# The two halves of every moving row of two MLPs are set 8 columns out of a 64-column step

## The chip, the core and the metric

The kernel runs on one core of one Trainium2 chip. Its engines are TensorE (PE for the matrix products, PEld for loading the stationary operand), VectorE (DVE), ScalarE (ACT), GpSimd (POOL) and SyncE (SP, which issues the DMAs). They work on SBUF, a memory of 128 partitions; PSUM holds the results of the matrix products. A column is here four bytes of a partition. The metric is the time of one execution on the chip in microseconds, the median over runs: 617.85 us before the change, from three runs of 614.94, 617.85 and 618.59 us.

## What is computed

Attention over a sliding window with a few sinks, and behind it two MLPs on the 1536 tokens:

```python
a = softmax(where(is_sink | in_window, q @ k.T / sqrt(64), -1e9))   # 2 batches, 8 heads, 768 tokens
x = (a @ v) as 1536 x 512
h = x @ w_in;  g = h * clip(h + 3, 0, 6) / 6;       x = g @ w_out    # first MLP, 512 -> 2048 -> 512
h = x @ w_in2; g = h / (1 + exp(-1.702 * h));       return g @ w_out2
```

All of it is in float32.

## The kernel before

**Exact products from three.** PE takes operands of the type F32R. Each float32 operand of the MLPs is split into a high part (a cast to F32R, by `copy`, lines 428 to 432) and a low part (the float32 value less the high one, a subtraction on VectorE), and each product is three matmuls: high by high, high by low, low by high. So x stands in `xyh` and `xyl` (lines 141 and 142, three blocks of 512 tokens each, four chunks of 128 features by 512 columns), a tile of W_in in `w0h` and `w0l`, a tile of W_out in `w1h` and `w1l`, and g in `gh` and `gl` (512 columns each).

**The stages.** The work is a list of 96 items: an item is one of 16 tiles of 128 inner features, for one block of 512 tokens, in one of the two MLPs. `up` (line 529) splits W_in's tile and makes 12 matmuls of 512 columns (four chunks by three products, line 541) into a bank of PSUM, forms u = h times its gate from it, and splits u into `gh` and `gl` (lines 578 to 587). `down` (line 592) makes 12 more (line 609) with W_out's parts. In the first MLP `gh` and `gl` are moving and W_out stationary there; in the second it is the other way round. `result` (line 625) writes x for the second MLP back into `xyh` and `xyl`.

**Moving rows.** A moving row of 512 columns is not read from left to right: `woven` (line 434) reads it as column 0, column 256, column 1, column 257 and so on, the two halves in turn. The results come out in that order, and W_out of the second MLP and the output's rows are laid out accordingly.

```python
    def woven(x):
        return x.rearrange("p (a n) -> p n a", a=2)
```

Every such row starts at a multiple of 64 columns in SBUF: two unused tiles, `gap_x` of 40 columns ahead of `xyh` and `gap_w` of 72 ahead of the MLP's tiles, see to that.

**Unpacking the weights.** A tile of weights comes by DMA as 2048 columns of 32-bit words into one of two `stage` tiles; a low and a top word of each weight stand side by side. `plan_convert` (line 445) makes 1024 float32 weights of it in `wf`, in five operations: the absolute value of the top words on ScalarE (L452), a clamp and a shift with a mask on `wf` (L457, L465), and two operations that take the top and then the low words in (L473, L480), these four on VectorE. L452, L473 and L480 read `stage` with a step of two columns:

```python
        wd = st.tile.rearrange("p (n t) -> p n t", t=2)
        low, top = wd[:, :, 0], wd[:, :, 1]
```

The 16 tiles of the first MLP are unpacked while the attention still runs, those of the second during the last items of the first MLP. From `wf` each item splits what it needs anew.

**What sets the order.** `Plan` collects operations with their reads, writes, the engines that may take them and an estimated cost, and `issue` (line 354) puts them out engine by engine in an order that follows from these costs and due times. Each engine works through its own list in that order. Tiles used in turn are rings of buffers (`mlp_rings`, line 679).

## Time and profile before

| | us |
|---|---|
| median of 3 runs (lowest, highest) | 617.85 (614.94, 618.59) |
| profiled execution | 615.07 |
| its span, first to last instruction | 613.3 |
| PE busy with matmuls | 586.0 |
| VectorE busy | 451.3 |
| ScalarE busy | 360.8 |
| mean share of PE's clock granted | 0.992 |

The span is the part of the execution from the first to the last instruction of the trace. Busy time is the time in which at least one instruction of the engine was under way. Consecutive matmuls overlap, and the mean time of one is longer than its distance from the next; the distance is read by counting matmuls in a stretch without gaps. A count with x in front belongs to the group or stretch; in a stretch it includes instructions that its ends cut. The sign <- behind an idle time names what ended it.

### The profile page before, as it was taken

To read this page: it belongs to the slowest core of one execution; us is meant where nothing else is said; L and a number is where in the kernel's file an instruction comes from. 1 tells how busy PE (TensorE), PEld (TensorE's weight loads), DVE (VectorE), ACT (ScalarE), POOL (GpSimd) and SP (SyncE) were. 2 spreads that over 40 slices of the span, in tenths; PEclk is the share of its full clock that TensorE was granted. 3 is DMA by queue.
4 is the path that set the end of the run, shared out by engine and by line. 5 is a ranking of instruction groups with operands and counts; after the bars stand their busy time and mean duration, and the time that the engine had idled before them with its cause. 6 is when DMAs were issued, how large, how long until landed. Compare 5 with 4: busy or idle time off the path is not lost.

```text
span 613.3 us, 10624 instructions
## 1 busy us (share of the span) xinstructions
PE 586.0 (96%) x4242; PEld 500.3 (82%) x4242; DVE 451.3 (74%) x896; ACT 360.8 (59%) x718; POOL 1.4 (0%) x10
## 2 busy tenths in 40 slices
PE   6889999999999999999999999999999999999995
PEld 6778777787878888888878877888888888888884
DVE  7799999999995665499999999945455455455541
ACT  5897776865765764475666575544644444544442
POOL 0000000000000000000000000000000000000000
PEclk9899999999999999999999999999999999999998
DMA  8974344244430000003444334000100000200002
GB/s 265 373 231 150 131 137 155 97 160 166 131 134 1 1 2 2 0 1 137 138 137 138 137 113 161 3 0 1 51 18 0 2 1 1 69 0 1 0 1 73
DMA packets 11175, 50.91 MB, mean 83 GB/s; under 512 B 1456, under 2 KB 1456, under 8 KB 7024
## 3 DMA queue, kind: packets, MB, share of 16 engines
q1 hardware_dynamic: 11120, 50.18, 24.6%
q8 instruction: 35, 0.57, 0.4%
q14 instruction: 20, 0.16, 0.1%
HBM read 47.02 MB, written 3.15 MB: 82 GB/s over the span
## 4 chain that ended last, share of the span: by engine, by line
PE 53%; DVE 30%; ACT 6%; DMA 6%; issue 5%; POOL 0%; SPq 0%; DVEq 0%; ACTq 0%; POOLq 0%
PE bank L609 24%; PE bank L541 24%; DMA stage<-in_w_dram 5%; DVE wf L480 5%; DVE wf L473 4%; DVE w1l L522 3%; DVE w0l L522 3%; DVE gl L584 3%; DVE u L558 3%; DVE wf L457 2%; ACT pexp L779 2%; ACT wf L452 2%; DVE wf L465 2%; DVE pexp L771 2%; PE bank L756 1%
## 5 line engine op out<-in xcount | busy, mean ns | idle before, releaser
L541 PE MATMUL bank<-xyh,w0h 128*128 128x512 f32 x384 | 147.1, 383 | 0.5 <-ACT xyh L430 0.5
L541 PE MATMUL bank<-xyl,w0h 128*128 128x512 f32 x384 | 145.7, 379 | 1.0 <-DVE xyl L857 1.0
L541 PE MATMUL bank<-xyh,w0l 128*128 128x512 f32 x384 | 145.7, 379 | 0.2 <-DVE w0l L522 0.2
L522 DVE TENSOR_TENSOR w1l<-wf,w1h 128x512 fp32r<-128x512 f32 x96 | 66.0, 687 | 56.9 <-ACT w1h L430 56.9
L430 ACT CAST w1h<-wf 128x512 fp32r<-128x512 f32 x90 | 55.6, 618 | 58.5 <-PE bank L609 57.7
L430 ACT CAST gh<-u 128x512 fp32r<-128x512 f32 x91 | 56.3, 619 | 44.4 <-DVE u L558 24.8
L541 PEld LDWEIGHTS bank<-xyl,w0h 128*128 128x128 f32 x384 | 72.6, 189 | 11.1 <-DVE xyl L857 1.3
L541 PEld LDWEIGHTS bank<-xyh,w0h 128*128 128x128 f32 x384 | 72.6, 189 | 10.9 <-issue 0.6
L541 PEld LDWEIGHTS bank<-xyh,w0l 128*128 128x128 f32 x384 | 72.6, 189 | 10.8 <-DVE w0l L522 0.6
L609 PE MATMUL bank<-gl,w1h 128*128 128x512 f32 x192 | 74.4, 388 | 4.0 <-DVE gl L584 3.7
L609 PE MATMUL bank<-w1h,gl 128*128 128x512 f32 x192 | 73.4, 382 | 2.0 <-DVE gl L584 1.9
L609 PE MATMUL bank<-gh,w1h 128*128 128x512 f32 x192 | 75.0, 391 | 0.2
L609 PE MATMUL bank<-w1h,gh 128*128 128x512 f32 x192 | 72.9, 380 | 0.0
L609 PE MATMUL bank<-w1l,gh 128*128 128x512 f32 x192 | 72.8, 379 | 0.0
L609 PE MATMUL bank<-gh,w1l 128*128 128x512 f32 x192 | 72.8, 379 | 0.0
L584 DVE TENSOR_TENSOR gl<-u,gh 128x512 fp32r<-128x512 f32 x96 | 66.2, 689 | 7.0 <-ACT gh L430 2.7
L572 DVE TENSOR_TENSOR u<-bank,u 128x512 f32<-128x512 f32 x48 | 32.9, 685 | 47.5 <-ACT u L567 47.5
L522 DVE TENSOR_TENSOR w0l<-wf,w0h 128x512 fp32r<-128x512 f32 x96 | 65.5, 682 | 1.7 <-ACT w0h L430 1.5
L567 ACT ACTIVATE u<-bank 128x512 f32<-128x512 f32 x48 | 28.7, 598 | 57.1 <-PE bank L541 57.1
L452 ACT ACTIVATE wf<-stage 128x1024 f32<-128x1024 f32 x32 | 47.1, 1472 | 20.2 <-DMA stage<-in_w_dram 19.2
L430 ACT CAST w0h<-wf 128x512 fp32r<-128x512 f32 x84 | 51.4, 612 | 0.7 <-DVE wf L480 0.4
L553 ACT ACTIVATE u<-bank,three 128x512 f32<-128x512 f32 x48 | 32.8, 684 | 31.7 <-PE bank L541 31.6
(93 smaller groups left out, 817.4 us busy)
## 6 DMA issues: line engine op xcount, KB each, us to landing
stage<-in_w_dram SPq DMA_DIRECT2D x32, 1024.0 KB, 5.0
wf<-in_kq_dram SPq DMA_DIRECT2D x8, 520.0 KB, 11.1
vc<-in_vc_dram SPq DMA_DIRECT2D x12, 320.0 KB, 6.6
out_dram<-u SPq DMA_DIRECT2D x12, 256.0 KB, 2.9
vb<-in_v_dram SPq DMA_DIRECT2D x10, 256.0 KB, 6.6
kq<-in_kq_dram SPq DMA_DIRECT2D x4, 520.0 KB, 10.8
vb<-in_v_dram SPq DMA_DIRECT2D x4, 128.0 KB, 6.4
par_i<-in_params_dram SPq DMA_DIRECT2D x1, 2.0 KB, 3.0
```

Source lines behind the costliest of these rows:

```text
L430: eng.copy(out, in_)
L452: lambda e: e.activation(w.tile.bitcast(F32), top.bitcast(F32), AF.Abs),
L473: lambda e: e.scalar_tensor_tensor(out=w.tile, in0=top, scalar=-0x40000000, in1=w.tile, op0=ALU.bitwise_and, op1=ALU.bitwise_or),
L480: lambda e: e.scalar_tensor_tensor(out=w.tile, in0=low, scalar=29, in1=w.tile, op0=ALU.logical_shift_right, op1=ALU.bitwise_or),
L522: lambda e: e.tensor_tensor(out=lo.tile, in0=src.tile.bitcast(F32)[:, cols], in1=hi.tile.bitcast(F32), op=ALU.subtract),
L541: e.matmul(h.tile[:, :n], w, woven(x), start=(c == 0 and k == 0), stop=(c == NC - 1 and k == 2))
L553: lambda e: e.activation(u.tile[:, :n], h.tile[:, :n], AF.Relu, bias=three, scale=1.0),
L558: lambda e: e.scalar_tensor_tensor(out=u.tile[:, :n], in0=u.tile[:, :n], scalar=6.0, in1=h.tile[:, :n], op0=ALU.min, op1=ALU.mult,),
L567: lambda e: e.activation(u.tile[:, :n], h.tile[:, :n], AF.Sigmoid, scale=1.702),
L572: lambda e: e.tensor_tensor(out=u.tile[:, :n], in0=h.tile[:, :n], in1=u.tile[:, :n], op=ALU.mult),
L584: lambda e: e.tensor_tensor(out=gl.tile[:, :n], in0=u.tile[:, :n], in1=gh.tile[:, :n].bitcast(F32), op=ALU.subtract),
L609: e.matmul(yb.tile, l, woven(r), start=(begin and k == 0), stop=(end is not None and k == 2))
```

## The change

x moves into one tile, `xy`, and W_out's parts and g's parts into one tile, `wg`. Each has two planes, one for the first halves of all rows and one for the second halves. The planes lie a multiple of 64 columns and 8 more apart: 6144 + 8 = 6152 columns in `xy` (six high and low blocks by four chunks by 256), 2048 + 8 = 2056 in `wg` (eight buffers of 256). Before, the two halves of a row lay 256 columns apart. `xy` begins at a multiple of 64 columns like `xyh` before it, `wg` at 16 columns more, and the other tiles behind `xy` move by 16 or 32 columns.

What writes these tiles now writes two pieces of 256 columns instead of one of 512 (four pieces of 128 from the attention, as before). A stationary operand of 128 columns out of them lies within one plane (`quarter`). Numbers, engines, estimated costs and the order of the instructions are as before on all five engines. W_in's parts `w0h` and `w0l`, which are stationary only, keep their form.

```diff
+APART = 8
...
     const.tile([P, 40], F32, name="gap_x")
-    xyh = [const.tile([P, NC, 512], F32R, name=f"xyh{s}") for s in range(NBLK)]
-    xyl = [const.tile([P, NC, 512], F32R, name=f"xyl{s}") for s in range(NBLK)]
+    xy = const.tile([P, 2, 2 * NBLK * NC * 256 + APART], F32R, name="xy")
+    xyh, xyl = (
+        [
+            xy[:, :, (2 * s + k) * NC * 256 : (2 * s + k + 1) * NC * 256].rearrange("p a (c n) -> p a c n", c=NC)
+            for s in range(NBLK)
+        ]
+        for k in range(2)
+    )
     landed = {}
...
     def woven(x):
-        return x.rearrange("p (a n) -> p n a", a=2)
+        return x.rearrange("p a n -> p n a")
+
+    def parted(x):
+
+        return x.rearrange("p (a n) -> p a n", a=2)
+
+    def quarter(x, e4):
+
+        return x[:, e4 // 2, e4 % 2 * P : (e4 % 2 + 1) * P]
     def halves(t0, n):
         return range(t0 // 256, (t0 + n) // 256)
...
             hi, lo = Buf(cls=f"w{part}h"), Buf(cls=f"w{part}l")
             cols = slice(512 * part, 512 * (part + 1))
             src = plan.wf[f]
+            of = lambda: parted(src.tile.bitcast(F32)[:, cols]) if part else src.tile.bitcast(F32)[:, cols]
             when = None
             plan.op(
                 to_act,
-                lambda e: copy(e, hi.tile, src.tile.bitcast(F32)[:, cols]),
+                lambda e: copy(e, hi.tile, of()),
                 when, reads=[src], writes=[hi], chain=f"split{part}",
             )
             plan.op(
                 [("DVE", 602)],
                 lambda e: e.tensor_tensor(
-                    out=lo.tile, in0=src.tile.bitcast(F32)[:, cols], in1=hi.tile.bitcast(F32), op=ALU.subtract
+                    out=lo.tile, in0=of(), in1=hi.tile.bitcast(F32), op=ALU.subtract
                 ),
                 when, reads=[src, hi], writes=[lo],
             )
...
             which, t0, n, f = items[i][:4]
             wh, wl = split(i, 0)
             h = Buf(cls="bank", kind="h")
-            s, o = divmod(t0, 512)
+            s = t0 // 512
+            assert n == 512 and t0 % 512 == 0
             for c in range(NC):
                 def mm(e, c=c):
-                    xh, xl = xyh[s][:, c, o : o + n], xyl[s][:, c, o : o + n]
+                    xh, xl = xyh[s][:, :, c, :], xyl[s][:, :, c, :]
                     cols = slice(c * P, (c + 1) * P)
                     prods = ((wh.tile[:, cols], xh), (wh.tile[:, cols], xl), (wl.tile[:, cols], xh))
                     for k, (w, x) in enumerate(prods):
...
                 )
             plan.op(
                 [("ACT", 520)] if i >= second - NF + 4 else [("ACT", 520), ("DVE", 335)],
-                lambda e: copy(e, gh.tile[:, :n], u.tile[:, :n]),
+                lambda e: copy(e, gh.tile, parted(u.tile)),
                 after, reads=[u], writes=[gh],
             )
             plan.op(
                 [("DVE", 602 if big else 335)],
                 lambda e: e.tensor_tensor(
-                    out=gl.tile[:, :n], in0=u.tile[:, :n], in1=gh.tile[:, :n].bitcast(F32), op=ALU.subtract
+                    out=gl.tile, in0=parted(u.tile), in1=gh.tile.bitcast(F32), op=ALU.subtract
                 ),
                 after, reads=[u, gh], writes=[gl],
             )
...
                 yb = ys["b"][e4]
                 def mm(e, e4=e4, yb=yb):
-                    col = slice(e4 * P, (e4 + 1) * P)
                     if which == 1:
-                        a, b = wh.tile[:, col], wl.tile[:, col]
+                        a, b = quarter(wh.tile, e4), quarter(wl.tile, e4)
                         prods = ((a, gh.tile), (b, gh.tile), (a, gl.tile))
                     else:
-                        prods = ((gh.tile[:, col], wh.tile), (gh.tile[:, col], wl.tile), (gl.tile[:, col], wh.tile))
+                        a, b = quarter(gh.tile, e4), quarter(gl.tile, e4)
+                        prods = ((a, wh.tile), (a, wl.tile), (b, wh.tile))
                     for k, (l, r) in enumerate(prods):
                         e.matmul(yb.tile, l, woven(r), start=(begin and k == 0), stop=(end is not None and k == 2))
...
         def result(which, t0, e4, yb, when):
             if which == 1:
                 s = t0 // 512
-                hi, lo = xyh[s][:, e4, :], xyl[s][:, e4, :]
+                hi, lo = xyh[s][:, :, e4, :], xyl[s][:, :, e4, :]
                 his = [plan.x[half][e4][0] for half in halves(t0, 512)]
                 los = [plan.x[half][e4][1] for half in halves(t0, 512)]
                 if (t0, e4) in kept_y:
...
                         when, reads=[psum], writes=[part],
                     )
                     yb = part
-                plan.op([("ACT", 478)], lambda e: e.mul(hi, yb.tile, 1.0 / 6.0), when, reads=[yb], writes=his)
+                plan.op([("ACT", 478)], lambda e: e.mul(hi, parted(yb.tile), 1.0 / 6.0), when, reads=[yb], writes=his)
                 plan.op(
                     [("DVE", 602)],
                     lambda e: e.scalar_tensor_tensor(
-                        out=lo, in0=yb.tile, scalar=1.0 / 6.0, in1=hi.bitcast(F32), op0=ALU.mult, op1=ALU.subtract,
+                        out=lo, in0=parted(yb.tile), scalar=1.0 / 6.0, in1=hi.bitcast(F32), op0=ALU.mult, op1=ALU.subtract,
                     ),
                     when, reads=[yb] + his, writes=los,
                 )
...
         down(len(items) - 1)
     def mlp_rings(plan, pool, psum):
+        parts = (("w1h", 2), ("w1l", 2), ("gh", NG), ("gl", NG))
+        n = sum(n for _, n in parts)
+        wg = pool.tile([P, 2, n * 256 + APART], F32R, name="wg")
+        k0 = 0
+        for cls, n in parts:
+            plan.ring(cls, n, lambda k, k0=k0: wg[:, :, (k0 + k) * 256 : (k0 + k + 1) * 256])
+            k0 += n
         for cls, n, cols, dt in (
-            ("w0h", 2, 512, F32R), ("w0l", 2, 512, F32R), ("w1h", 2, 512, F32R),
-            ("w1l", 2, 512, F32R), ("u", NU, 512, F32), ("gh", NG, 512, F32R), ("gl", NG, 512, F32R), ("aside", 4, 512, F32),
+            ("w0h", 2, 512, F32R), ("w0l", 2, 512, F32R), ("u", NU, 512, F32), ("aside", 4, 512, F32),
         ):
             plan.ring(cls, n, lambda k, cls=cls, cols=cols, dt=dt: pool.tile([P, cols], dt, name=cls, tag=f"{cls}{k}"))
         plan.ring("bank", 8, lambda k: psum.tile([P, 512], F32, name="bank", tag=f"bank{k}"))
...
                 [("PE", 2000)], values, when, reads=list(dict.fromkeys([rows] + halves_of)) + pts, writes=[av],
             )
             blk, off = divmod(T, 4)
-            dst = (slice(None), slice(None), slice(off * P, (off + 1) * P))
+            dst = (slice(None), off // 2, slice(None), slice(off % 2 * P, (off % 2 + 1) * P))
             late = when + 500
             src = lambda: av.tile.rearrange("p (n t) -> p n t", n=NPAIR)
             his = [plan.x[T // 2][c][0] for c in range(NC)]
```

No instruction stands elsewhere than before; two excerpts show what is different in a row. The first is VectorE's list where a weight tile of the first MLP is unpacked, before (`gl` is the low part of g, `w1h` and `w1l` are W_out's parts; in brackets the engines waited for):

```order
L473 SCALAR_TENSOR_TENSOR wf_66<-stage_60,wf_66 128x1024 [waits DMAHW7_49]
L584 TENSOR_TENSOR gl<-u,gh 128x512 [waits Activation_49]
L480 SCALAR_TENSOR_TENSOR wf_66<-stage_60,wf_66 128x1024 [waits DVE_49]
L457 TENSOR_SCALAR wf_67<-wf_67 128x1024
L432 CAST w1h<-wf_66 128x512 [waits DVE_49,PE_49]
```

The same place after it, with the line numbers of the changed kernel:

```order
L489 SCALAR_TENSOR_TENSOR wf_66<-stage_60,wf_66 128x1024 [waits DMAHW7_49]
L602 TENSOR_TENSOR wg<-u,wg 128x2x256 [waits Activation_49]
L496 SCALAR_TENSOR_TENSOR wf_66<-stage_60,wf_66 128x1024 [waits DVE_49]
L473 TENSOR_SCALAR wf_67<-wf_67 128x1024
L440 CAST wg<-wf_66 128x2x256 [waits DVE_49,PE_49]
```

Only the tile and the shape of what is written differ. The second is PE's list after the change, in the first MLP at the start of a sum over tiles of inner features, whose four banks of PSUM are written for the first time here:

```order
L627 MATMUL bank<-wg 128x512 [waits Activation_49]
L627 MATMUL bank<-wg 128x512
L627 MATMUL bank<-wg 128x512 [waits DVE_49]
L627 MATMUL bank<-wg 128x512 [waits PE_49]
L627 MATMUL bank<-wg 128x512 x5
L627 MATMUL bank<-wg 128x512 [waits PE_49]
```

The waits of PE on its own earlier matmuls are new there; the path that runs has eight of them more than before, each on a matmul 31 to 73 matmuls back.

## Rows read from the trace of the kernel before

**Rows 1.** The page: busy time and share by engine, clock by slice.
```profile
PE 586.0 (96%) x4242; PEld 500.3 (82%) x4242; DVE 451.3 (74%) x896; ACT 360.8 (59%) x718; POOL 1.4 (0%) x10
...
PEclk9899999999999999999999999999999999999998
```
**Rows 2.** Five stretches of the span: busy us (instructions) by engine, granted clock, DMA.
```profile
core 0: us, PE busy (x) PEld busy (x) DVE busy (x) ACT busy (x) POOL busy (x), PEclk, DMA share, GB/s
0.00:41.00 41.00, 32.37 (x754) 28.74 (x754) 31.53 (x152) 31.77 (x104) 1.42 (x10) 0.92 0.91 300
41.00:180.00 139.00, 132.91 (x1389) 109.03 (x1384) 135.38 (x312) 97.48 (x223) 0.00 (x0) 1.00 0.43 142
180.00:264.00 84.00, 83.70 (x565) 72.30 (x566) 49.19 (x104) 49.31 (x103) 0.00 (x0) 1.00 0.02 9
264.00:395.00 131.00, 125.65 (x567) 105.54 (x566) 130.44 (x170) 82.69 (x120) 0.00 (x0) 1.00 0.33 113
395.00:613.30 218.30, 211.37 (x980) 184.65 (x978) 104.78 (x161) 99.50 (x171) 0.00 (x0) 0.99 0.05 15
```
**Rows 3.** Two stretches of the second MLP, same columns.
```profile
420.00:500.00 80.00, 80.00 (x373) 70.06 (x372) 41.43 (x64) 38.72 (x67) 0.00 (x0) 1.00 0.04 14
500.00:580.00 80.00, 80.00 (x372) 70.09 (x371) 39.52 (x61) 37.34 (x65) 0.00 (x0) 1.00 0.05 14
```
**Rows 4.** Groups from 264 to 395 us: busy us, mean ns, idle before, releaser.
```profile
L609 PE MATMUL bank<-gl,w1h 128*128 128x512 f32 x68 | 26.7, 392 | 3.4 <-DVE gl L584 3.4
...
L452 ACT ACTIVATE wf<-stage 128x1024 f32<-128x1024 f32 x16 | 24.5, 1532 | 9.3 <-DMA stage<-in_w_dram 8.4 <-DVE w1l L522 0.8
L480 DVE SCALAR_TENSOR_TENSOR wf<-stage,wf 128x1024 int32<-128x1024 int32 x16 | 24.5, 1528 | 0.1
L473 DVE SCALAR_TENSOR_TENSOR wf<-stage,wf 128x1024 int32<-128x1024 int32 x16 | 24.3, 1521 | 0.3
...
L430 ACT CAST gh<-u 128x512 fp32r<-128x512 f32 x23 | 14.2, 618 | 18.8 <-DVE u L558 12.4 <-DVE u L572 6.3
...
L609 PE MATMUL bank<-w1h,gl 128*128 128x512 f32 x26 | 10.4, 399 | 2.0 <-DVE gl L584 1.9
```
**Rows 5.** Operations by line, min/median/max ns: gl; w0l twice, w1l; L457 twice.
```profile
L584 DVE TENSOR_TENSOR gl<-u,gh x96: 655/691/760, 49.5 to 603.2; 128x512 fp32r<-128x512 f32 x96
...
L522 DVE TENSOR_TENSOR w0l<-wf,w0h x19: 656/681/732, 289.4 to 391.3; 128x512 fp32r<-128x512 f32 x19
...
L522 DVE TENSOR_TENSOR w1l<-wf,w1h x31: 684/692/693, 419.9 to 573.4; 128x512 fp32r<-128x512 f32 x31
...
L522 DVE TENSOR_TENSOR w0l<-wf,w0h x31: 679/681/691, 421.1 to 576.5; 128x512 fp32r<-128x512 f32 x31
...
L457 DVE TENSOR_SCALAR wf<-wf x2: 661/674/686, 23.8 to 36.3; 128x1024 f32<-128x1024 f32 x2
...
L457 DVE TENSOR_SCALAR wf<-wf x13: 668/684/733, 295.3 to 386.8; 128x1024 f32<-128x1024 f32 x13
```
**Rows 6.** The reads of stage, same columns: outside the stream, in it, whole run.
```profile
L480 DVE SCALAR_TENSOR_TENSOR wf<-stage,wf x3: 1216/1218/1222, 32.7 to 53.4; 128x1024 int32<-128x1024 int32 x3
...
L480 DVE SCALAR_TENSOR_TENSOR wf<-stage,wf x14: 1505/1523/1590, 292.7 to 391.9; 128x1024 int32<-128x1024 int32 x14
...
L473 DVE SCALAR_TENSOR_TENSOR wf<-stage,wf x14: 1498/1518/1545, 290.0 to 389.3; 128x1024 int32<-128x1024 int32 x14
...
L473 DVE SCALAR_TENSOR_TENSOR wf<-stage,wf x32: 1215/1506/1581, 26.1 to 389.3; 128x1024 int32<-128x1024 int32 x32
...
L452 ACT ACTIVATE wf<-stage x2: 1147/1163/1179, 19.7 to 28.7; 128x1024 f32<-128x1024 f32 x2
...
L452 ACT ACTIVATE wf<-stage x7: 1293/1604/1642, 305.9 to 350.3; 128x1024 f32<-128x1024 f32 x7
```
**Rows 7.** Writes in four pieces and in one; VectorE's casts. Same columns.
```profile
L857 DVE TENSOR_TENSOR xyl<-bank,xyh x12: 673/680/692, 19.4 to 216.0; 128x512 fp32r<-128x512 f32 x12
...
L642 DVE SCALAR_TENSOR_TENSOR xyl<-bank,xyh x8: 675/684/692, 223.8 to 359.5; 128x512 fp32r<-128x512 f32 x8
...
L432 DVE CAST w0h<-wf x12: 395/419/470, 34.2 to 178.3; 128x512 fp32r<-128x512 f32 x12
L432 DVE CAST w1h<-wf x6: 416/420/427, 73.2 to 188.0; 128x512 fp32r<-128x512 f32 x6
L432 DVE CAST gh<-u x5: 395/419/422, 48.9 to 180.9; 128x512 fp32r<-128x512 f32 x5
```
**Rows 8.** Groups of the whole run by line: busy us, mean ns, idle before, releaser.
```profile
L480 DVE SCALAR_TENSOR_TENSOR wf<-stage,wf 128x1024 int32<-128x1024 int32 x32 | 47.3, 1479 | 0.2
L452 ACT ACTIVATE wf<-stage 128x1024 f32<-128x1024 f32 x32 | 47.1, 1472 | 20.2 <-DMA stage<-in_w_dram 19.2 <-DVE w1l L522 0.8
L473 DVE SCALAR_TENSOR_TENSOR wf<-stage,wf 128x1024 int32<-128x1024 int32 x32 | 46.7, 1460 | 0.3
```

More of the change, by code (lines that the diff above doesn't have):

```diff
@@ L689, in put_x @@
         blk, off = divmod(T, 4)
-        dh = xyh[blk][:, :, off * P : (off + 1) * P]
+        at = (slice(None), off // 2, slice(None), slice(off % 2 * P, (off % 2 + 1) * P))
+        dh = xyh[blk][at]
         nc.scalar.copy(dh, x)
         nc.vector.tensor_tensor(
-            out=xyl[blk][:, :, off * P : (off + 1) * P], in0=x, in1=dh.bitcast(F32), op=ALU.subtract
+            out=xyl[blk][at], in0=x, in1=dh.bitcast(F32), op=ALU.subtract
         )
```

## The prediction

> **What bounds the kernel now.** [...] One busy share over stages hides who waits, so I cut the span into five stretches [rows 2]. In three of them PE sets the time: from 180 to 264 us and from 395 us to the end it is busy nearly throughout while VectorE is at about half. In the other two it is VectorE: from 41 to 180 us it is busy 135.4 of 139.0 us, from 264 to 395 us 130.4 of 131.0 us, and PE has gaps. These are the two stretches in which the 16 weight tiles of each MLP are unpacked from `stage` (L452 on ScalarE, L457 to L480 on VectorE).
>
> Next I asked what a 512-column matmul costs where nothing disturbs it [rows 3]: 745 in 160 us, 0.215 us each. [...] In the stretch from 264 to 395 us 567 matmuls begin or end, which is 121.9 us of the 131.0: PE lacks 9.1 us there, and what it waits for is `gl`, written by VectorE [rows 4].
>
> Is anything slowed by PE's reading? I compared operations inside the matmul stream with the same ones outside it. Most do not change: `w0l` takes a median of 681 ns in both MLP stretches, `gl` 655 to 760 over the whole run, the contiguous 1024-column clamp L457 674 ns without the stream and 684 with it [rows 5]. Three lines do change, and they are the ones that read `stage` with a step of two columns: L480 takes 1218 ns without the stream and 1523 with it, L473 1518 with it (its minimum, 1215, is L480's), the Abs L452 1163 without and 1604 with it [rows 6].
>
> **A reading of that stretch.** VectorE's 512-column operation takes 681 ns and its 1024-column one 1218, so 537 ns are for 512 columns and 144 are fixed. A strided read of one tile passes over 2048 columns of `stage`: without the stream in 1218 - 144 = 1074 ns, 1.91 columns per ns; in the stream in 1523 - 144 = 1379 ns, 1.49 per ns. PE passes 256 columns of each half in 215 ns, 1.19 per ns. If PE's two halves keep one place of a 64-column cycle occupied, a faster reader that catches up is held behind it, and gets past once per matmul, in the seam between two: then it gains 64 columns per matmul, (256 + 64) / 215 = 1.49 per ns. That is the row's speed. ScalarE's Abs, with the same 144 ns (no row gives its own), goes at 2.01 free and 1.40 held. Two readers of unlike speed brought to nearly the same one is what holding would look like. An operation slower than 1.19 per ns, as all 512-column ones are (512 / 537 = 0.95), never runs up from behind, and those are not stretched. L457 passes 1024 columns in about 540 ns and is not stretched either, which speaks against this reading unless it reads in two parts. [...]
>
> **The change part by part.** No instruction is added, removed or moved on any engine. Eight matmuls of the path that runs get a wait of PE on itself (the excerpt in the section on the change); each waits for a matmul 31 or more before it, 31 x 0.215 = 6.7 us earlier, so it is long met: 0. Three waits of VectorE on PE fall away, which another wait had covered: 0. `xy` and `wg` end 16 columns later each; the fixed `w0h`, `u` and mask tiles shift by 16 or 32 columns. No row shows an effect of that; 0.
>
> *Writes in two pieces.* Casts and subtractions now write 2 x 256 columns. The nearest rows are L857, which writes 4 x 128 (median 680), against L642, which writes 512 in one piece (684): no price [rows 7]. VectorE's fast cast (420 ns) has no row with pieces: 11 of its 23 casts (`w1h`, `gh`) write into `wg`. From below 0, from above the 684 ns of the slower kind, 11 x 0.264 = 2.9 us. I take 0, as pieces cost L857 nothing.
>
> *The strided reads.* This is the term that decides. Excess now: L480 47.3 us and L473 46.7 us against 32 x 1.218 = 39.0 each is 8.3 + 7.7 = 16.0 us of VectorE; L452 47.1 against 32 x 1.163 = 37.2 is 9.9 us of ScalarE [rows 8]. From 264 to 395 us it is 24.5 + 24.3 - 39.0 = 9.8 us of VectorE and 24.5 - 18.6 = 5.9 of ScalarE [rows 4], so the first unpacking holds 6.2 and 4.0. With the halves 8 columns apart in the 64-column cycle, each of two places gets half of PE's reads where one got all. No row has such halves. Bounds: the excess goes wholly (free speed), or a reader is held by both places and no longer gets past (1.19 per ns: 2048 / 1.19 + 144 = 1865 ns, +342 each). I take the first: a place that PE reads in every second column leaves the other to the reader, and the rows show no sign that PE's reading closes a place for longer than its own access, since 512-column operations, which PE overtakes, pay at most 10 ns.
>
> *What it is worth.* From 264 to 395 us VectorE would fall to 130.4 - 9.8 = 120.6 us, just below PE's 121.9; so PE becomes the bound and at most its 9.1 us come back. With two engines that close, in-order waits between them remain (ScalarE's cast of `gh` waits 18.8 us for `u` there [rows 4]); I take 7. From 41 to 180 us VectorE is busy 97%, its 6.2 us bound the gain, and part of PE's gaps there belong to the attention's short matmuls; I take 4.5. ScalarE's share lies beside VectorE's, 0. Elsewhere PE sets the time: 0. Sum 11.5 us: the profiled execution, 615.07 us with 613.3 of span, would come to 603.6. It stands 2.8 us under the median of the runs shown, 617.85, so the forecast for a median is 606.
>
> **The rivals.** *No effect.* The stretch could be a share of the memory's rate taken by PE, wherever its halves lie: both readers end near 1.4 to 1.5 columns per ns, which a fixed share would also do. For it: the figure of one lap per matmul may be chance. Against: contiguous readers pay nothing. Time 618. [...]
>
> *Half the effect.* The reader still loses a little at each of two places: half of 11.5, time 612.
>
> *Two closed places (slower).* If any read by PE closes a place, two are closed, and the seam between matmuls is too short to get past both. L473 and L480 rise by 342 ns: 32 x 0.342 = 10.9 us in the second unpacking, where VectorE is the bound; in the first, 6.2 us of excess at 305 each are 20 wholly covered reads, 7 us, of which 5 reach the end. Time 634. It decides from about 0.13 us more per read.
>
> *PE itself slows.* Every matmul row of this trace has its halves in step; out of step is not shown. 2304 matmuls give 2.3 us per ns, so 3 ns more would make it slower by over 1%. For it there is only the absence of a row; at 5 ns, time 629 if nothing else moved.
>
> **How the numbers follow.** The whole effect 0.50 (606), half 0.12 (612), none 0.18 (618), two closed places 0.13 (634), a slower PE 0.07. About 1%, 6.2 us, is what a measurement here tells from no change. Faster by over 1% is under 611.7: the first case, 0.50. Within 1%: half and none, 0.30. Slower: 0.20. The range leaves out the last two: up to 621, no effect with the casts' 2.9 us; down to 600, where all 9.1 us of the second stretch, all 6.2 of the first and some of ScalarE's 4.0 come back. The likeliest case alone runs from 600 to 610.
>
> **What would show it.** L480 and L473 near 1218 ns and L452 near 1163 from 290 to 395 us; 512-column matmuls still at 0.215 us; VectorE no longer at 99% from 264 to 395 us, PE without gaps there; casts at 420 ns. It is wrong if the three strided lines keep their 1.5 and 1.6 us, if they exceed 1.8, or if matmuls in an undisturbed stretch take longer than 0.215 us.

## The result and the profile after

The changed kernel takes 601.54 us (median of four runs, 600.42 to 602.81) where the kernel before, on the same chip, takes 617.12 (four runs): a ratio of 0.9751, 95% interval 0.9714 to 0.9788. That is faster by 15.6 us, inside the predicted range and 4.5 us below the predicted 606. The profiled execution took 602.81 us, with a span of 601.0.

The page of the changed kernel, busy time by engine and the chain that ended last:

```profile
span 601.0 us, 10621 instructions
...
PE 580.4 (97%) x4242; PEld 502.5 (84%) x4242; DVE 435.8 (73%) x896; ACT 352.4 (59%) x718; POOL 1.4 (0%) x10
...
PE 83%; DVE 8%; ACT 4%; DMA 3%; issue 1%; POOL 0%; SPq 0%; POOLq 0%; ACTq 0%
```

Against [rows 1] VectorE lost 15.5 us of work and ScalarE 8.4, with as many instructions (896 and 718). The predicted excess was 16.0 and 9.9. The lines that read `stage` (L452, L473 and L480 are now L468, L489 and L496), groups of the changed kernel's whole run, as in [rows 8]:

```profile
L489 DVE SCALAR_TENSOR_TENSOR wf<-stage,wf 128x1024 int32<-128x1024 int32 x32 | 39.1, 1222 | 0.3
L496 DVE SCALAR_TENSOR_TENSOR wf<-stage,wf 128x1024 int32<-128x1024 int32 x32 | 39.1, 1221 | 0.2
L468 ACT ACTIVATE wf<-stage 128x1024 f32<-128x1024 f32 x32 | 37.9, 1186 | 16.9 <-DMA stage<-in_w_dram 13.5 <-DMA vb<-in_v_dram 2.5 <-DVE wg L539 0.8
```

They now cost beside the matmul stream what they cost without it in [rows 6] (1218 and 1163 ns); of Abs's excess 0.02 us a tile is left. The five stretches of the changed kernel, columns as in [rows 2]:

```profile
core 0: us, PE busy (x) PEld busy (x) DVE busy (x) ACT busy (x) POOL busy (x), PEclk, DMA share, GB/s
0.00:41.00 41.00, 32.64 (x748) 29.02 (x749) 31.46 (x151) 31.84 (x104) 1.42 (x10) 0.92 0.91 300
41.00:180.00 139.00, 133.79 (x1411) 112.27 (x1408) 133.18 (x327) 98.13 (x235) 0.00 (x0) 1.00 0.45 147
180.00:264.00 84.00, 84.00 (x565) 73.06 (x564) 49.09 (x96) 48.37 (x95) 0.00 (x0) 1.00 0.00 1
264.00:395.00 131.00, 131.00 (x608) 114.36 (x607) 123.87 (x175) 80.39 (x125) 0.00 (x0) 1.00 0.32 113
395.00:601.00 206.00, 198.95 (x922) 173.74 (x920) 98.20 (x151) 93.66 (x162) 0.00 (x0) 0.99 0.06 16
```

From 264 to 395 us PE has no gap left. It runs 608 matmuls there instead of 567, 41 more at 0.215 us, which is 8.8 us. VectorE is busy for 123.87 us of the 131 although more instructions fall into the stretch: it no longer sets the time. By 264 us the changed kernel has run 748 + 1411 + 565 = 2724 matmuls, the kernel before 2708. After 395 us both are without a matmul for about the same time, 6.9 us before and 7.1 after. So of the 12.3 us between the two spans 8.8 came from the second unpacking and 3.5 from what lies before it. The matmuls themselves did not change: 372 in the 80 us from 420 to 500, as in [rows 3].

```profile
420.00:500.00 80.00, 80.00 (x372) 70.07 (x371) 39.76 (x61) 37.10 (x64) 0.00 (x0) 1.00 0.05 14
```

### The profile page after: what moved, and what is told of

Same layout as the page of the kernel before. It is cut to its first block, busy times and chain, and to the rows that moved or that the text cites. A ratio compares the mean times of both kernels' runs of the same rounds, so it can differ in the third digit from the quotient of the medians.

```text
span 601.0 us, 10621 instructions
## 1 busy us (share of the span) xinstructions
PE 580.4 (97%) x4242; PEld 502.5 (84%) x4242; DVE 435.8 (73%) x896; ACT 352.4 (59%) x718; POOL 1.4 (0%) x10
## 4 chain that ended last, share of the span: by engine, by line
PE 83%; DVE 8%; ACT 4%; DMA 3%; issue 1%; POOL 0%; SPq 0%; POOLq 0%; ACTq 0%
PE bank L627 38%; PE bank L559 38%; DMA stage<-in_w_dram 3%; PE bank L781 2%; PE bank L832 2%; ACT pexp L804 2%; PE bank L855 2%; PE bank L863 1%; DVE wf L489 1%; DVE wf L496 1%; DVE pexp L796 1%; DVE u L576 1%; PE heat L178 1%; DVE wg L602 1%; DVE wg L539 1%
## 5 line engine op out<-in xcount | busy, mean ns | idle before, releaser
L627 PE MATMUL bank<-wg 128*128 128x512 f32 x1152 | 285.4, 381 | 1.5 <-ACT wg L438 1.3
L627 PEld LDWEIGHTS bank<-wg 128*128 128x128 f32 x1152 | 215.6, 189 | 34.4 <-ACT wg L438 2.0
L559 PE MATMUL bank<-xy,w0h 128*128 128x512 f32 x768 | 230.3, 381 | 1.5 <-DVE xy L882 1.0
L559 PEld LDWEIGHTS bank<-xy,w0h 128*128 128x128 f32 x768 | 143.9, 189 | 22.2 <-DVE xy L882 1.3
L559 PE MATMUL bank<-xy,w0l 128*128 128x512 f32 x384 | 145.5, 379 | 0.0
L539 DVE TENSOR_TENSOR wg<-wf,wg 128x512 fp32r<-128x512 f32 x96 | 66.1, 689 | 57.6 <-ACT wg L438 57.6
L559 PEld LDWEIGHTS bank<-xy,w0l 128*128 128x128 f32 x384 | 72.6, 189 | 10.3
L438 ACT CAST wg<-u 128x512 fp32r<-128x512 f32 x91 | 56.3, 619 | 31.7 <-DVE u L590 17.4
L602 DVE TENSOR_TENSOR wg<-u,wg 128x512 fp32r<-128x512 f32 x96 | 66.2, 689 | 6.9 <-ACT wg L438 2.7
L468 ACT ACTIVATE wf<-stage 128x1024 f32<-128x1024 f32 x32 | 37.9, 1186 | 16.9 <-DMA stage<-in_w_dram 13.5
L489 DVE SCALAR_TENSOR_TENSOR wf<-stage,wf 128x1024 int32<-128x1024 int32 x32 | 39.1, 1222 | 0.3
L496 DVE SCALAR_TENSOR_TENSOR wf<-stage,wf 128x1024 int32<-128x1024 int32 x32 | 39.1, 1221 | 0.2
```

Of the source, the lines that this page charges most:

```text
L438: eng.copy(out, in_)
L468: lambda e: e.activation(w.tile.bitcast(F32), top.bitcast(F32), AF.Abs),
L489: lambda e: e.scalar_tensor_tensor(out=w.tile, in0=top, scalar=-0x40000000, in1=w.tile, op0=ALU.bitwise_and, op1=ALU.bitwise_or),
L496: lambda e: e.scalar_tensor_tensor(out=w.tile, in0=low, scalar=29, in1=w.tile, op0=ALU.logical_shift_right, op1=ALU.bitwise_or),
L539: lambda e: e.tensor_tensor(out=lo.tile, in0=of(), in1=hi.tile.bitcast(F32), op=ALU.subtract),
L559: e.matmul(h.tile[:, :n], w, woven(x), start=(c == 0 and k == 0), stop=(c == NC - 1 and k == 2))
```

## The experiments

Four questions were open: whether the place of the halves does it or the new tiles; whether a read is held behind TensorE's reads or only gets a smaller share of a rate; which engine's reads are worth the time; and how far apart the halves must be. Each ratio is to the kernel before as it ran on the same chip (616.59, 616.53 or 615.64 us), and the brackets give its 95% interval.

**Back in step, new tiles kept.** The distance in the 64-column cycle goes back to zero and all else of the change stays.

```diff
-APART = 8
+APART = 0
```

> The changed kernel with 0 columns instead of 8: two planes, one tile for x and one for W_out's and g's parts, all halves a multiple of 64 columns apart. HOLDING: the reads of stage are back at 1.52 us (VectorE) and 1.60 us (ScalarE), the time at 617, ratio to the kernel before 0.998 to 1.003. TILES (the gain comes from the one tile, its writes in two planes or the shifted neighbours): the reads stay at 1.22 and 1.19 us and the time at 602.

Measured: 617.13 us, ratio 1.0006, 95% interval 0.9992 to 1.0020. Time and reads are back at what they were, as the holding theory had it:

```profile
L496 DVE SCALAR_TENSOR_TENSOR wf<-stage,wf 128x1024 int32<-128x1024 int32 x32 | 47.3, 1477 | 0.2
L489 DVE SCALAR_TENSOR_TENSOR wf<-stage,wf 128x1024 int32<-128x1024 int32 x32 | 46.9, 1465 | 0.3
L468 ACT ACTIVATE wf<-stage 128x1024 f32<-128x1024 f32 x32 | 46.8, 1463 | 21.0 <-DMA stage<-in_w_dram 20.0 <-DVE wg L539 0.8
```

So the whole gain is that of the 8 columns. The writes in two pieces, the planes in one tile and the changed waits are worth nothing that ten runs can see. The reads are what comes and goes with the gain.

**The read by itself.** A probe runs a stream of woven matmuls and, beside it, three reads of `stage` for each setting (its code, shortened):

```python
for d in (0, 1, 2, 4, 6, 8, 12, 16, 32, 48, 56, 60, 64, 72, 128, 192):
    m = const.tile([P, 2, 256 + d], F32R)           # halves 256 + d columns apart
    ...                                             # 33 matmuls on m, woven
    scalar_tensor_tensor(out=o, in0=stage.rearrange("p (n t) -> p n t", t=step)[:, :, step - 1], ...)
```

> No part of the kernel: a probe that leaves attention and MLPs out. A stream of matmuls with woven rows of known distance between the halves (256 columns and 0 to 192 more), and beside it three reads of a 2048-column tile at a time, by VectorE (the operation of L473) or ScalarE (Abs). HOLDING (PE's halves keep one place of 8 columns in a 64-column cycle occupied; a faster reader is held and gets past once per matmul): VectorE's step-2 read 1.52 us at 0, 64, 128 and 192 columns apart, 1.22 at 8, 12, 16, 32, 48, 56 and 72; at 1, 2, 4, 6 and 60 in between, in proportion to the overlap (1.49, 1.45, 1.37, 1.30, 1.37). In step, the reader's speed in columns is fixed, so step 4 (512 elements) and step 8 (256 elements) over the same 2048 columns take 1.52 us too, against 0.68 and 0.41 without the stream; matmuls of 256 columns let it past twice as often: (256 + 128) / 215 = 1.79 columns per ns, 1.29 us; matmuls of 128 columns 1.22. RATE SHARE (PE takes a part of the memory's rate; a reader pays per 16-byte piece it touches): 305 ns more at step 2 and at step 4 (0.99 us), half of it at step 8 (0.56), no change with the length of a matmul, and a distance between the halves can matter only through the pieces, so 4 columns apart are as good as 8. Both: contiguous reads 1.22 at any distance. Abs: 1.60 in step, 1.16 at 8 and 32.

Groups of the probe by line. The name of the result says the engine and by how many columns the halves are out of step, or the step of the read ("eight_step" with the halves 8 apart, else in step), or that matmuls have fewer columns (short), or that their rows lie in one piece (plain):

```profile
L95 ACT ACTIVATE act_apart_zero<-stage 128x1024 f32<-128x1024 f32 x3 | 4.7, 1574 | 0.1
...
L91 DVE SCALAR_TENSOR_TENSOR dve_apart_zero<-stage,wf 128x1024 int32<-128x1024 int32 x3 | 4.6, 1523 | 0.1
...
L91 DVE SCALAR_TENSOR_TENSOR dve_step_four<-stage,wf 128x512 int32<-128x512 int32 x3 | 4.6, 1521 | 0.1
...
L91 DVE SCALAR_TENSOR_TENSOR dve_short_half<-stage,wf 128x1024 int32<-128x1024 int32 x3 | 4.0, 1345 | 0.1
L91 DVE SCALAR_TENSOR_TENSOR dve_apart_one<-stage,wf 128x1024 int32<-128x1024 int32 x3 | 3.9, 1299 | 0.1
...
L91 DVE SCALAR_TENSOR_TENSOR dve_apart_two<-stage,wf 128x1024 int32<-128x1024 int32 x3 | 3.7, 1221 | 0.1
...
L91 DVE SCALAR_TENSOR_TENSOR dve_apart_eight<-stage,wf 128x1024 int32<-128x1024 int32 x3 | 3.7, 1221 | 0.1
L95 ACT ACTIVATE act_apart_eight<-stage 128x1024 f32<-128x1024 f32 x3 | 3.5, 1170 | 0.1
...
L91 DVE SCALAR_TENSOR_TENSOR dve_eight_step_four<-stage,wf 128x512 int32<-128x512 int32 x3 | 3.3, 1104 | 0.1
...
L91 DVE SCALAR_TENSOR_TENSOR dve_step_eight<-stage,wf 128x256 int32<-128x256 int32 x3 | 1.9, 620 | 0.1
```

The period is 64 columns: 0, 64, 128 and 192 columns all give 1521 to 1525 ns, and every distance from 2 to 60 gives 1221 to 1223. Matmuls alone do it, with no other work on the core. So a share of the rate that PE takes wherever its halves lie is out.

A fixed rate beside halves that are in step is not out by this alone. The two theories were to part at a step of four: such a read passes the same 2048 columns with half the elements and takes 1521 ns in step, the very time of the step of two. But with the halves 8 apart it takes 1104 ns and not the 0.68 us I had written, and a rate counted in pieces of 4 columns, of which both steps touch all 512, would give equal times as well. The step of eight speaks against such a rate: it touches every second piece, which would be (1523 - 144) / 2 + 144 = 834 ns, and takes 620, the same as with the halves 8 apart. A reader held behind a moving place would take what the place lets it, and by that theory the step of eight, 620 ns in step and out of it, puts the place under 8 columns. What I had wrong is that size: I had expected the step of eight to be held, and 2, 4, 6 and 60 columns to be half free (1.30 to 1.45 us).

Matmuls of 256 columns start every 112 ns in the trace (two series of 64 take 14.6 us together), so a reader that gains 64 columns in each passes (128 + 64) / 112 = 1.71 columns per ns: 2048 / 1.71 + 144 = 1339 ns, measured 1345. This sum was done afterwards; with 215 ns for two matmuls I had written 1.29 us. With 128 columns, which also start every 112 ns (128 in 14.5 us), the read is free (1221), as expected but not by that sum, which gives 1.9 us. TensorE then reads only half as many columns in the same time; whether that is why is not shown.

**Half of the change.** `xy` keeps its 8 columns, `wg` goes back into step.

```diff
-        wg = pool.tile([P, 2, n * 256 + APART], F32R, name="wg")
+        wg = pool.tile([P, 2, n * 256], F32R, name="wg")
```

> The changed kernel with only x's halves 8 columns out of step; those of W_out's and g's parts lie a multiple of 64 columns apart. Half of the moving rows are in step. HOLDING: reads of stage that fall beside matmuls with W_out's and g's parts stay at 1.5 us, those beside x at 1.22, the mean in the second unpacking near 1.37; VectorE gets half of its 9.8 us back there, and the time is 609 (607 to 612). If one half in step suffices to hold a reader through (it does not fall free again in the other half's turn): 614 to 617. If a reader once free stays ahead: 603.

Measured: 607.66 us, ratio 0.9859 (0.9823 to 0.9894), in the range expected. VectorE's reads take a mean of 1337 and 1330 ns over the whole run, which leaves 7.4 of their 16.0 us of excess, about half; in the second unpacking L489 takes from 1216 to 1539 ns, with a median of 1450. A read's time now depends on which matmuls run beside it. Two short windows of this kernel, each with one read by L489:

```profile
L489 DVE SCALAR_TENSOR_TENSOR wf<-stage,wf 128x1024 int32<-128x1024 int32 x1 | 1.2, 1216 | 0.0
L559 PE MATMUL bank<-xy,w0h 128*128 128x512 f32 x4 | 1.2, 379 | 0.0
L559 PE MATMUL bank<-xy,w0l 128*128 128x512 f32 x3 | 1.1, 379 | 0.0
...
L627 PE MATMUL bank<-wg 128*128 128x512 f32 x8 | 1.9, 379 | 0.0
L489 DVE SCALAR_TENSOR_TENSOR wf<-stage,wf 128x1024 int32<-128x1024 int32 x1 | 1.5, 1539 | 0.0
...
L468 ACT ACTIVATE wf<-stage 128x1024 f32<-128x1024 f32 x1 | 1.4, 1353 | 0.1
...
L559 PE MATMUL bank<-xy,w0l 128*128 128x512 f32 x1 | 0.4, 379 | 0.0
```

From 314.1 to 315.3 us it lies beside matmuls that stream `xy` and is free (1216 ns); from 321.6 to 323.1 it lies beside those that stream `wg` and is held (1539). This is the plainest sight of the mechanism in the kernel itself: the same instruction on the same kind of tile, seven microseconds apart, beside other moving rows. One more thing differs, ScalarE's Abs in the second window; by itself it holds nothing, for in the third probe below a read with such an Abs beside it and the halves 4 columns apart takes 1222 ns.

**VectorE alone, by another way.** The kernel before, halves in step, but L473 and L480 read 1024 columns in a row instead of every second one. The work is the same; what this kernel leaves out is the sorting of top and low words, so its weights are not the model's.

```diff
-                out=w.tile, in0=top, scalar=-0x40000000, in1=w.tile, ...
+                out=w.tile, in0=st.tile[:, :1024], scalar=-0x80000000, in1=w.tile, ...
...
-                out=w.tile, in0=low, scalar=29, in1=w.tile, ...
+                out=w.tile, in0=st.tile[:, 1024:], scalar=29, in1=w.tile, ...
```

> The kernel before, with VectorE's two reads of stage (L473, L480) taking 1024 words in a row instead of every second one, and the sign bit alone in L473; the weights come out wrong by it, the work is the same. ScalarE's Abs keeps its step of two. HOLDING: L473 and L480 go to 1.22 us although all halves are in step, Abs stays at 1.60 us, and nearly all of the change's gain appears without the change: 603 to 606, because VectorE is the engine that PE waits for. If the gain of the change does not come through these reads, the time stays at 617; if ScalarE's share carries a good part of it, 608 to 611.

Measured: 604.57 us, ratio 0.9810 (0.9781 to 0.9839), in the range expected.

```profile
L452 ACT ACTIVATE wf<-stage 128x1024 f32<-128x1024 f32 x32 | 47.5, 1484 | 17.8 <-DMA stage<-in_w_dram 17.0 <-DVE w1l L522 0.8
...
L473 DVE SCALAR_TENSOR_TENSOR wf<-stage,wf 128x1024 int32<-128x1024 int32 x32 | 39.0, 1219 | 0.3
...
264.00:395.00 131.00, 130.98 (x606) 113.64 (x605) 123.46 (x175) 85.42 (x125) 0.00 (x0) 1.00 0.32 113
```

VectorE is freed (1219 ns) while ScalarE stays held (1484), and from 264 to 395 us PE runs 606 matmuls without a gap, as good as all of the change's 608. There ScalarE's excess is indeed covered. The 0.4 to 0.6% by which this kernel's ratio lies above the changed kernel's is at the edge of the intervals; if it is real, some 3 us are ScalarE's, before 264 us. The profiled executions show less: by 264 us this kernel has run 2719 matmuls, the changed one 2724 and, profiled again, 2729, which is 1 to 2 us.

**How wide the held place is.** A second probe lets the row of every matmul start some columns later in the cycle than the one before, and reads in other steps.

```python
m[:, :, n * k % 64 : n * k % 64 + 256].rearrange("p a n -> p n a")   # row k starts n * k columns into the cycle, halves in step
```

> A second probe without the kernel's work, built like the first one: three reads of a 2048-column tile beside a stream of 512-column matmuls at 216 ns, halves in step unless said. Two questions. (a) Each moving row starts j columns later in the 64-column cycle than the one before it. HOLDING BEHIND PE says that a held reader gains in each 216 ns the 256 columns that PE passes and what the next row jumps ahead, or one whole lap of 64 where it starts in place (j = 0) and the reader slips past in the seam: VectorE 144 + 2048 x 216 / (256 + j), so 1.53 us at j = 0 and, worse, 1.82 at 8, 1.77 at 16, 1.68 at 32, 1.60 at 48, 1.56 at 56; at 4 either 1.84 or, if it still slips past, 1.5. ScalarE's Abs (1.57 at j = 0): 1.87 at 8, 1.73 at 32, 1.61 at 56. FIXED RATE (a reader beside rows in step gets a fixed rate, wherever PE is) says 1.53 and 1.57 at every j. (b) The place that is held is a piece of 4 columns: a reader whose next element lies one piece further runs into PE again, one that skips a piece gets past. So step 3 is held (1.52 us), steps 5, 6 and 7 take within 10% of what they take with no matmuls beside them; a place of one or two columns would free step 3 too, a place of 8 would hold steps 5 to 7 (1.5 us). Halves 3, 62 columns apart: 1.22 us as at 2; 63 as at 1, 1.30; Abs at 1: 1.16 to 1.35.

```profile
L86 DVE SCALAR_TENSOR_TENSOR dve_later_thirtytwo<-stage,wf 128x1024 int32<-128x1024 int32 x3 | 5.0, 1662 | 0.1
...
L86 DVE SCALAR_TENSOR_TENSOR dve_later_fortyeight<-stage,wf 128x1024 int32<-128x1024 int32 x3 | 4.8, 1601 | 0.1
...
L86 DVE SCALAR_TENSOR_TENSOR dve_step_three<-stage,wf 128x682 int32<-128x682 int32 x3 | 4.6, 1528 | 0.1
...
L86 DVE SCALAR_TENSOR_TENSOR dve_later_zero<-stage,wf 128x1024 int32<-128x1024 int32 x3 | 4.6, 1523 | 0.1
L86 DVE SCALAR_TENSOR_TENSOR dve_later_fiftysix<-stage,wf 128x1024 int32<-128x1024 int32 x3 | 4.6, 1520 | 0.1
...
L86 DVE SCALAR_TENSOR_TENSOR dve_later_eight<-stage,wf 128x1024 int32<-128x1024 int32 x3 | 4.5, 1489 | 0.1
...
L86 DVE SCALAR_TENSOR_TENSOR dve_step_five<-stage,wf 128x409 int32<-128x409 int32 x3 | 2.8, 944 | 0.1
```

Where the next row starts changes the read's time, as holding wants and a fixed rate cannot: at 32 and 48 columns the read gets slower still, 1662 and 1601 ns, where a gain of only the shift gives 1680 and 1599. At 8 and 16 columns I had written 1.82 and 1.77 us and measured 1489 and 1468 ns. There the reader gets past as it does at zero and gains the shift on top, (256 + 64 + 8) / 216 = 1.52 per ns or 1493 ns, and 1460 at 16; at 4 it gives 1509, measured 1507. So my sum was wrong for small shifts, and this extension was found afterwards. At 56 and 60 columns neither sum fits VectorE: a gain of only the shift gives 1562 and 1544 ns, measured are 1520 and 1527, no slower than at zero. A step of three is held (1528 ns), a step of five all but free (944 ns, 902 with little beside it). So the place looks like a piece of about 4 columns, 16 bytes, that a reader in steps of up to four (1521 ns at four, in step) cannot step over. Two small distances missed what I had written: 63 columns take 1491 ns (1.30 us expected), and Abs at 1 column 1440 (at most 1.35).

**Two columns, and eight again.** If pieces of 4 columns were all, 2 columns should not quite separate the halves, but the first probe had them free.

```diff
-APART = 8
+APART = 2
```

> The changed kernel with the planes a multiple of 64 columns and 2 (instead of 8) apart. The first probe had the reads of stage undisturbed at 2 columns: reads at 1.22 and 1.19 us, time as with 8, 602, within 0.5% of the changed kernel run beside it. If the whole kernel's rows need the full 8: reads above 1.3 us and over 606.

> The changed kernel as it is, beside e4 and for a closer look at the size of the gain. By the stages of the two profiles that exist (12.3 us: 3.9 in the first unpacking, 8.6 in the second) the ratio would be 0.980; by the medians 0.975. If the gain in the medians is larger because executions of the kernel before differ by what their first stretch loses, the ratio stays near 0.976 and the spans of single runs show a spread of over 1 us in each kernel.

Measured on one chip: with 2 columns 609.29 us, ratio 0.9894 (0.9869 to 0.9919), where I had expected 602 by the first probe; with 8 again 601.88 us, ratio 0.9774 (0.9751 to 0.9796), whose interval just leaves out the 0.980 of the two profiles. The kernel with 2 columns:

```profile
L468 ACT ACTIVATE wf<-stage 128x1024 f32<-128x1024 f32 x32 | 43.5, 1360 | 18.2 <-DMA stage<-in_w_dram 17.3 <-DVE wg L539 0.8
...
L496 DVE SCALAR_TENSOR_TENSOR wf<-stage,wf 128x1024 int32<-128x1024 int32 x32 | 42.2, 1318 | 0.2
...
264.00:395.00 131.00, 129.76 (x590) 110.12 (x590) 126.89 (x173) 82.59 (x123) 0.00 (x0) 1.00 0.31 113
```

Some 40% of the excess of VectorE's reads over the whole run stays, some 60% of Abs's, and 23 of the 41 matmuls come back. The first probe had told too little.

**Four columns; and why two are not enough.** The first is the changed kernel with `APART = 4`. The second is a probe of the same read at 0, 2, 4 and 8 columns, alone (only) and with what the kernel has beside it: an Abs on ScalarE (withabs), a cast, a result written in place, moving and stationary operands that change (weights).

> The changed kernel with the halves 4 columns more than a multiple of 64 apart in place of 8. Theory (a place that a read of TensorE holds is a piece of 4 columns, 16 bytes; with 2 columns the two halves still share a piece half of the time, with 4 never): the strided reads of DVE take 1.22 us and Abs 1.19 us as with 8 columns; time 602 us (601 to 604), ratio 0.977. Rival (in the whole kernel the place is wider than 4 columns, as the stretched reads at 2 columns suggest): the reads keep a good part of the stretch, 1.27 us or more on DVE, and the time is 604 to 609 us, ratio 0.983 or more.

> A probe that leaves the kernel's work out: reads of stage in steps of two columns beside woven matmuls, with the halves 0, 2, 4 and 8 columns out of step, (a) alone, (b) with an Abs in steps of two on ScalarE at the same time on another tile, (c) with a contiguous cast of ScalarE, (d) with the result written onto its own second operand, (e) with stationary operands and moving rows that change from matmul to matmul, (f) with all of it. It asks why 2 columns freed such a read in the first probe (1.22 us) and only half freed it in the kernel (1.32 us). At 0 columns every read of DVE should take 1.52 us, at 4 and 8 columns 1.22 us. At 2 columns: if a second reader is what matters, (b) and (f) rise to 1.30 to 1.40 and (a), (c), (d), (e) stay at 1.22; if changing rows matter (their starts lie 256 columns apart, the same in the cycle of 64), (e) and (f) rise; if the result in place matters, (d) and (f). If none of them rises, it is something of the kernel that the probe still lacks.

Measured: with 4 columns 601.82 us, ratio 0.9779 (0.9741 to 0.9816), with reads of 1222 and 1220 ns and Abs at 1179: as good as 8. Groups of the probe by line:

```profile
L82 DVE SCALAR_TENSOR_TENSOR withabs_two<-stage,wf 128x1024 int32<-128x1024 int32 x3 | 4.3, 1429 | 0.1
L82 DVE SCALAR_TENSOR_TENSOR only_two<-stage,wf 128x1024 int32<-128x1024 int32 x3 | 4.2, 1404 | 0.1
...
L82 DVE SCALAR_TENSOR_TENSOR withabs_four<-stage,wf 128x1024 int32<-128x1024 int32 x3 | 3.7, 1222 | 0.1
```

At 0 columns the read takes 1524 ns here too. None of my causes is it by itself: at 2 columns the read takes 1404 ns with only the matmuls beside it, where the first probe had 1221, and 1378 to 1441 with one of the others. All of them at once add some (a median of 1497), but they are not what holds it. What differs between the two probes with only the matmuls beside the read is, as far as their code shows, how their rows lie, so one more took that apart, with all rows in one tile: the first half at its column 0, 4 or 8 (at_zero, at_four, at_eight), the second 258 (quarter), 322 (cycle), 514 (half), 770 (third), 1026 (one) or 2050 (two) columns on.

> A probe that leaves the kernel's work out: the same strided read of stage beside woven matmuls, all of whose rows lie in one tile. It separates the two things in which the first and the third probe differ at 2 columns out of step (1.22 us there, 1.40 us here, where the matmuls also took 217 in place of 216 ns): the distance from half to half (258 columns there, 1026 here) and the column at which the rows start (8 more there, counted in a cycle of 16). Start theory: quarter_at_zero and one_at_zero (258 and 1026 columns, the third probe's start) both read in 1.40 us, quarter_at_eight and one_at_eight (the first probe's start) both in 1.22. Distance theory: quarter reads in 1.22 us at every start; one and two (1026 and 2050) in 1.40 at every start, and half (514), third (770) and cycle (322) tell where it turns. At 4 columns out of step (apart_four) 1.22 us at every distance, or 4 columns too would depend on it; in step 1.52 us at both distances.

```profile
L64 DVE SCALAR_TENSOR_TENSOR one_at_zero<-stage,wf 128x1024 int32<-128x1024 int32 x3 | 4.3, 1426 | 0.1
...
L64 DVE SCALAR_TENSOR_TENSOR two_at_eight<-stage,wf 128x1024 int32<-128x1024 int32 x3 | 4.2, 1407 | 0.1
...
L64 DVE SCALAR_TENSOR_TENSOR quarter_at_zero<-stage,wf 128x1024 int32<-128x1024 int32 x3 | 4.1, 1364 | 0.1
...
L64 DVE SCALAR_TENSOR_TENSOR quarter_at_eight<-stage,wf 128x1024 int32<-128x1024 int32 x3 | 3.7, 1223 | 0.1
L64 DVE SCALAR_TENSOR_TENSOR one_at_eight<-stage,wf 128x1024 int32<-128x1024 int32 x3 | 3.7, 1223 | 0.1
...
L64 DVE SCALAR_TENSOR_TENSOR two_apart_four<-stage,wf 128x1024 int32<-128x1024 int32 x3 | 3.7, 1222 | 0.1
```

At 2 columns the start decides, and the distance hardly: from column 0 the read is held at every distance (1364 to 1426 ns), from columns 4 and 8 it is free at 258 and 1026 (1222 and 1223). One row speaks against a rule by the start alone: 2050 columns from column 8, 1407 ns. And two columns the other way (318 and 1022) are free from column 0 (1223). Why a start should matter stays open, and so does the asymmetry of 63 columns (1491 ns in the second probe) against 1 (1299 to 1318 in three probes). What the kernel needs is settled: 4 columns are free at all three distances of this probe (1222 ns), and in the kernel (1222 and 1220).

## Why the prediction was right, and where its sizes were off

- **What bounds the kernel** held. Each stretch in which VectorE set the time got shorter and no other did, and the share of VectorE in the chain that ended last fell from 30 to 8%, while PE's rose from 53 to 83%. The chain of the kernel before, to set beside the one above:

```profile
PE 53%; DVE 30%; ACT 6%; DMA 6%; issue 5%; POOL 0%; SPq 0%; DVEq 0%; ACTq 0%; POOLq 0%
```

- **The strided reads are held, not rationed.** A share of the rate wherever the halves lie fails at the result itself, at the distances of the first probe and at the two windows of the kernel with half of the change. A fixed rate beside halves in step fails at the step of eight (620 ns) and at the shifted rows (1662 ns). One lap of 64 columns gained per matmul, the prediction's figure, comes out again beside matmuls of 256 columns (1339 ns by the sum, 1345 measured). What is not accounted for are the matmuls of 128 columns, the shifts of 56 and 60, the odd cases at 1 and 2 columns, and L457: it passes 1024 columns in about 540 ns, 1.90 per ns against PE's 1.19, and is not held (674 ns without the stream, 684 in it [rows 5]). That it reads in two parts no run shows. By the steps of three (1528 ns) and five (944) the place is some 4 columns wide, smaller than the 8 with which the first probe was planned, which changed nothing at a distance of 8.
- **"The excess goes wholly"** was right: 39.1, 39.1 and 37.9 us against the 39.0, 39.0 and 37.2 of the sum. The rival of two closed places would have shown 1.87 us a read.
- **The second unpacking** was put at 7 of PE's 9.1 us and gave 8.8. (PE's idle time there was 5.4 us, 131.0 less 125.65 in [rows 2], nearly all of it for `gl`; the rest of the 9.1 shows only in the count of matmuls.) I kept back 2 us for in-order waits among two engines that close. VectorE has 7 us of slack there (131.0 less 123.87), and PE finds its operands ready: the waits shrank with the work they stood behind. The mechanism was right, the deduction was not needed.
- **The first unpacking** was put at 4.5 us. The two profiled executions give 3.5 together with all that lies before 180 us. Executions of one kernel differ as much there: by 264 us the kernel before had run 2708 matmuls and its twin, the kernel back in step, 2693; the changed kernel 2724, and 2729 when profiled again. With 4 columns, whose reads take as long, it is 2747. What is left after 264 us are 512-column matmuls, so these counts put the term between 3 and 12 us. The medians, less 8.8, leave 6 to 7 us; it is not known better.
- **From the profiled execution to the median.** Of the 4.5 us by which 606 was missed, 0.8 is the sum (11.5 against 12.3); the rest is this step. The profiled execution of before, 615.07, is near its fastest (614.94), that of the changed kernel, 602.81, its slowest. Profile against profile the gain is 12.3 us, close to the 11.5 of the sum; medians give 15.6. I carried a gain from one execution over to a median as if their difference were fixed. That the two profiled executions come so close to the sum is in part luck.
- **The terms put at nothing** came to nothing that shows. Casts by VectorE into two pieces take 419 to 420 ns as in [rows 7], the subtraction into two pieces a median of 691 as in [rows 5], and the eight new waits of PE on itself show in no gap. The 0 where PE sets the time supposed that a matmul there gets no shorter, which no row of before shows; in the changed kernel it is 0.215 us still, 372 in the 80 us from 420 to 500. A row for the casts, of the changed kernel by line (min, median and max ns):

```profile
L440 DVE CAST wg<-wf x6: 416/420/426, 72.8 to 184.2; 128x512 fp32r<-128x512 f32 x6
```

- **ScalarE's share at nothing** holds from 264 to 395 us; before that, up to 3 us may be ScalarE's, by the run in which VectorE reads in a row.
- **The range's low end** of 600 stood for both stretches giving all they had and ScalarE some of its 4.0 us besides. The measured 601.5 lies only 1.5 us above it. In the second unpacking the deduction was not needed; for the first the runs can't tell. That the range held owes something to luck: it allowed for all of both stretches, not for the difference between the executions profiled and the medians.
- **The rival of no effect**, 618 us, fell: beside matmuls alone, in the first probe, Abs takes 1574 ns with the halves in step and 1170 with them 8 apart, and VectorE's read 1523 and 1221.

## What to carry to other kernels

When an instruction costs more inside a stream of matmuls than outside it, and its neighbours of other strides don't, compare the columns per nanosecond at which each passes over its tile with TensorE's: readers of unlike speed that come down to nearly one speed (here from 1.91 and 2.01 to 1.49 and 1.40) may be held behind it, and then where the moving rows lie decides it. Moving the halves apart, in the kernel or in a probe, tells. Rows read as two interleaved halves should not have the halves a multiple of 64 four-byte columns apart (1521 to 1525 ns a read in the first probe); in these runs 4 columns more free the readers (1220 to 1222 ns), and 2 do not always (1221 in the first probe, 1404 in the third). Price such a change by the stretches in which the held engine sets the time, and take several executions before carrying a difference of 2 us over to a median.

## What had not been expected of the hardware

- Halves 2 columns out of step can cost the matmuls themselves a little. In the third probe 204 matmuls keep TensorE busy for 45.3 us with 2 columns and 45.0 with 8, the read beside them being held with 2 (1404 ns) and free with 8 (1223). In the kernel such a cost hardly shows: from 395 to 600 us TensorE is busy for 203.94 us with 943 matmuls at 2 columns and for 198.95 us with 922 at 8, 0.2163 against 0.2158 us each.
- In the first probe a row in one piece holds no reader (1222 and 1151 ns), but streams slower than a woven one, 15.3 us against 14.1 for 64 matmuls each:

```profile
L81 PE MATMUL work<-mplain,st 128*128 128x512 f32 x64 | 15.3, 395 | 0.0
L81 PE MATMUL work<-mtwo,st 128*128 128x512 f32 x64 | 14.1, 379 | 0.0
```

- A free read of VectorE in steps costs neither by its columns nor by its elements alone. With the halves 8 apart, steps of two, four, eight and sixteen over the same 2048 columns (1024, 512, 256 and 128 elements) take 1221, 1104, 620 and 370 ns; 1024 elements in a row take 1222.
